# Start of a sketched-attention and ReGLU kernel: order of the first loads, filler matmuls, and the form of the stores

## Chip, cores, metric

The kernel runs on one core of a Trainium2 chip. The metric is the device time of one execution in microseconds; smaller is better. All times below are microseconds (us) unless marked otherwise, and places in a trace are counted from the start of the span.

## What is computed

Attention with polynomial sketch features, then a feed-forward layer with a gate. Cut to what matters:

```python
# q, k, v: (4 batches, 4 heads, 1088 tokens, 32); S1, S2: (8, 32), all float32
def phi(x):                                   # 64 features of a token
    a, b = S1 @ x, S2 @ x                     # 8 and 8
    return outer(a, b).reshape(64)
kv  = sum over tokens of phi(k) v^T           # per batch and head: 64 x 32
z   = sum over tokens of phi(k)
att = (phi(q) @ kv) / (phi(q) @ z + 1e-6)
x   = att, heads side by side                 # (4352 tokens, 128)
out = (relu(x @ w_gate) * (x @ w_val)) @ w_out   # d_ff = 1536, out (4352, 128)
```

## The kernel before, in words

The 4352 tokens are cut into 136 columns of 32 tokens (34 to a batch). They are worked on in nine groups: one of 8 columns, eight of 16. The feed-forward part of a group runs in "pairs": a pair is 1024 columns of hidden units times tokens, three pairs in the first group, six in each other one, 51 in all. One pair is a gate product on TensorE (gate, L553, into two PSUM tiles), two ReLU evacuations on ScalarE (relu, L566), a value product on TensorE (val, L553), their elementwise product on VectorE (prod, L570), and eight output matmuls that accumulate into o_ps (outp, L579). At the end of a group ScalarE copies o_ps to o_sb (oevac, L585), and SyncE (SP) stores it (store, L588 to L605). The first group's tokens take a quarter of the hidden units' 12 blocks of 128 in each pair, so the third pair is the first that reads blocks 8 to 11 of the gate and value weights.

Before a batch's tokens can be used, its keys go through class K (L258): transposes of k on VectorE (t1q, L319; t1r for the 64 rest keys, L315), sketches on TensorE (L330), a transpose back (t2, L350), key sums (zsum, L364), their masked copy zm on VectorE (zevac, L370), the product with S1 (w, L377) and its evacuation to wst on ScalarE (wevac, L382), the outer products that make the key features (phi, L249, on VectorE and GpSimd), and the key-value matmuls (kv, L389) with their evacuation to kv_bd (kvevac, L396). In batch 0 the value rows arrive as float32 (v32) and are cast on ScalarE (L307) ahead of wevac. A group's queries go through class Q (L418 on): transpose (L459), sketch with wst (L468), transpose back (L475), the denominator (L485 to L493), the features (L497, L249), a transpose on TensorE (tr, L509), its copy on ScalarE (L513), the product with kv_bd (num, L521) and the copy to xT (L528), which the gate product reads.

All of these, and most loads, are handed to a planner (class Plan, L21 to L76) as operations with an engine, a planned duration, dependencies and a due time. It plays them through once and emits each engine's instructions in the order of the planned starts; on the chip every engine runs its own list strictly in that order. So planned durations and landing times (the lists `land` and `qland`, L533 to L538) set orders, and only orders. Where the plan leaves TensorE idle in the head, the loop at L655 to L660 puts in filler matmuls on a tile of zeros (warm, L218 to L220); 48 more stand at the start (L222).

DMA issues before the planner (L163 to L197): the first keys on SP's and ScalarE's queues, then S1 and S2 (s16, 4 KB each), the rest keys (kR), 8 columns of q, the values; on GpSimd's queue, whose loads cast to float16, two thirds of the gate and value weights, and behind a mask two thirds of the output weights. The remaining thirds and the later batches' values are planned on GpSimd (L632 to L650), the later keys and queries on SP. The transposes of S (L225, L230) follow the 48 fillers on TensorE; skS and S1bd (L227, L232) are made of them on VectorE, ahead of the key transposes.

Of the kernel before, what the change touches and what calls it, by code (L numbers as in the profile page):

```python
# [79 lines left out]
def kernel(  # L80
# [12 lines left out]
    nc = tc.nc  # L93

    B, H, S, D = q.shape
# [4 lines left out]
    NJ = DF // 128  # L100
# [37 lines left out]
    def load_k(eng, b, h):  # L138
        eng.dma_start(out=kA[b][32 * h:32 * h + 32].rearrange("t b q d -> t b (q d)"),
                      in_=k[b, h, 0:1024, :].rearrange("(b t q) d -> t b (q d)", b=4, q=8))  # L140

    def load_kr(eng, b):
        eng.dma_start(out=kR[b], in_=k[b, :, 1024:, :].rearrange("h (t e) d -> h t (e d)", e=2))
# [5 lines left out]
    def load_vr(eng, dst, b):  # L149
        eng.dma_start(out=dst[0:64, :, 8, :], in_=v[b, :, 1024:, :].rearrange("h p d -> p h d"))  # L150
# [8 lines left out]
    def load_wo(lo, hi):  # L159
        nc.gpsimd.dma_start(  # L160
            out=wo[:, lo:hi], in_=moe_w_out.rearrange("(j f) m -> f j m", f=128)[:, lo:hi])

    load_k(nc.sync, 0, 0)  # L163
    load_k(nc.scalar, 0, 1)
    load_k(nc.sync, 0, 2)
    load_k(nc.scalar, 0, 3)
    nc.scalar.dma_start(out=s16[0:R], in_=S1[:, None, :].to_broadcast([R, 4, D]))
    nc.sync.dma_start(out=s16[R:2 * R], in_=S2[:, None, :].to_broadcast([R, 4, D]))
    load_kr(nc.sync, 0)
    nc.sync.dma_start(out=qA[:, 0:8, :],  # L170
                      in_=q[0].rearrange("h (t n) d -> h t n d", n=NT)[:, :, 0:8, :].rearrange(
                          "h t n d -> h t (n d)"))
    load_vr(nc.sync, v32, 0)

    zero = sb("zero", [128, 128], FP16)
    nc.vector.memset(zero, 0.0)
    scr = sb("scr", [1, 1], FP16)
    nc.scalar.activation(out=scr, in_=zero[0:1, 0:1], func=ACTF.Relu)
    load_v(nc.scalar, v32, 0)

    id32 = sb("id32", [2 * R, 2 * R])
    make_identity(nc, id32)
# [11 lines left out]
    load_w(wv, moe_w_val, 0, 8)  # L194
    ident = sb("ident", [128, 128], FP16)
    make_identity(nc, ident)
    load_wo(0, 8)  # L197

    z32 = sb("z32", [128, 32])
    mask2 = sb("mask2", [128, 2])  # L200
# [216 lines left out]
    class Q:  # L417


        def __init__(self, g, land):  # L420
            self.g = g
            n0, nn = self.n0, self.nn = groups[g]
            self.parts = parts(n0, nn)
            bs = [b for b, _, _ in self.parts]
            m = self.m = nn // 2
            self.qT = rot("qT", g, 4, [128, 16, 32])[:, 0:nn]
            self.ab = rot("abq", g, 4, [128, 8, 2, 32])[:, 0:m]
            self.qp = rot("qp", g, 4, [128, 8, 2, R * R], FP16)[:, 0:m]
# [12 lines left out]
            e = "DVE" if g == 0 else "POOL"  # L441
            d1 = P.add(e, 0.25 if g == 0 else 0.45, lambda: self.bwm(e), [t2])
            d2 = P.add("DVE", 0.15 + 0.15 * f, self.red, [d1])
            d3 = P.add("DVE", 0.2, self.rec, [d2])
            d4 = P.add(e, 0.25 if g == 0 else 0.42, lambda: self.am(e), [d3])
            if g == 0:
                ph = [P.add("DVE", 0.62, lambda: self.phi(0, 3, "DVE"), [d4]),
                      P.add("POOL", 0.42, lambda: self.phi(3, 4, "POOL"), [d4])]
            else:
                ph = [P.add("POOL", 0.15 + 0.226 * 4, lambda lo=lo: self.phi(lo, lo + 4, "POOL"), [d4])  # L450
                      for lo in (0, 4)]
            tr = P.add("PE", 0.47 * f, self.tr, ph, take=("M", n + "t"), lat=0.2)
            te = P.add("ACT", 0.15 + 0.85 * f, self.tre, [tr], give=(n + "t",))
            nu = P.add("PE", 0.2 + 0.25 * f, self.num, [te, *(kk[b].kvx for b in bs)],
                       take=("M", n + "x"), lat=0.25)
            self.xx = P.add("ACT", 0.15 + 0.46 * f, self.x, [nu], give=(n + "x",), due=need - 0.6)
# [73 lines left out]
                    "p (a t s) -> p a t s", a=4, s=ns),  # L530
                in_=m_ps[:, 0:32 * self.nn].rearrange("p (a s t) -> p a t s", a=4, s=ns))

    kk = [K(0, [4.8, 4.8, 4.8, 4.8, 7.2, 5.3], [0, 4, 9], [("DVE", "POOL"), ("POOL", "POOL")])]  # L533
    qland = [6.3, 16.0, 20.0, 24.0]
    qq = [Q(0, qland)]
    for b in range(1, B):
        kk.append(K(b, [[0, 14.0, 18.0, 22.0][b]] * 2, [0, 5, 9], [("POOL", "POOL")] * 2))
    qland[0] = 9.0  # L538
    for g in range(1, 9):
        qq.append(Q(g, qland))  # L540

# [45 lines left out]
    def store(g):  # L587
        n0, nn = groups[g]  # L588
        ns = nn // 4
        t = o_t.pop(g)  # L590
        runs = []
        for a in range(4):
            at = n0 + a * ns
            b, l = divmod(at, NT)
            if l + ns > NT:
                runs += [(a, 1, 0, NT - l, b, l), (a, 1, NT - l, ns, b + 1, 0)]
            elif runs and runs[-1][4] == b and runs[-1][3] == ns and runs[-1][2] == 0:
                a0, c, lo, hi, b0, l0 = runs[-1]
                runs[-1] = (a0, c + 1, lo, hi, b0, l0)
            else:  # L600
                runs.append((a, 1, 0, ns, b, l))
        for a, c, lo, hi, b, l in runs:
            dst = out[b * S:(b + 1) * S].rearrange("(t n) m -> t n m", n=NT)
            dst = dst[:, l:l + c * (hi - lo), :].rearrange("t (a s) m -> a t (s m)", a=c)
            nc.sync.dma_start(out=dst, in_=t[32 * a:32 * (a + c), lo:hi, :].rearrange("p s m -> p (s m)"))  # L605

    rel, pro, ou, oe = [], [], [], {}
    lastpe = None
    for i, (g, y) in enumerate(pairs):
# [16 lines left out]
        if lst:  # L626
            oe[g] = P.add("ACT", 0.15 + 0.42 * groups[g][1] / 16, lambda g=g: oevac(g), [ou[-1]],
                          due=due + 4.6)
            P.add("SP", 0.4, lambda g=g: store(g), [oe[g]], due=due + 5.2)


    for eng, at, fn in [  # L632
        ("POOL", 9.0, lambda: load_w(wg, moe_w_gate, 8, NJ)),
        ("POOL", 9.1, lambda: load_w(wv, moe_w_val, 8, NJ)),
        ("POOL", 9.2, lambda: load_wo(8, NJ)),
        ("POOL", 9.3, lambda: load_v(nc.gpsimd, v_sb[1], 1)),
        ("POOL", 9.4, lambda: load_vr(nc.gpsimd, v_sb[1], 1)),
    ]:
        P.add(eng, 0.6, fn, at=at, due=at + 2.0)
# [9 lines left out]
            P.add("POOL", 0.8, lambda b=b: load_v(nc.gpsimd, v_sb[b], b), at=6.0 * b, due=8.0 * b)  # L649
            P.add("POOL", 0.6, lambda b=b: load_vr(nc.gpsimd, v_sb[b], b), at=6.0 * b, due=8.0 * b)  # L650

    order = P.run({"PE": 5.0, "DVE": 4.3, "ACT": 5.2, "POOL": 5.2, "SP": 6.0})
    pe = 5.0
    go = qq[0].xx["end"]
    for o in order:  # L655
        if o["eng"] == "PE":
            if o["start"] <= go + 0.5 and o["start"] - pe > 0.3:
                warm(int((o["start"] - pe - 0.15) * 0.8 / 0.056))
            pe = o["end"]
        o["fn"]()  # L660

# [29 lines left out]
```

## Time and profile before

| what | us |
|---|---|
| median of 3 runs (lowest, highest) | 124.31 (124.18, 124.97) |
| the profiled execution's own time | 123.37 |
| its span | 121.6 |
| busy: TensorE, VectorE, ScalarE, GpSimd | 108.7, 90.0, 75.4, 52.1 |
| first gate matmul starts | 20.69 |
| last output matmuls end | 114.13 |
| last store issued | 114.8 |
| DMA packets, bytes | 10527, 9.47 MB |

The profiled execution is shorter than the three timed runs; its rows are compared with its own time. Busy time of TensorE counts pipelined matmuls whose ends are modelled, so it says little about how much of the engine is used. "PEld" is a weight load. In timelines a row gives start, duration, engine and line, output and inputs, how many instructions were merged, and in brackets how long the engine was idle before and what ended that. A row of windows gives, for a stretch of time, the busy time of each engine with its instructions, then the granted TensorE clock (1.00 is full), the DMA engines' busy share (it can exceed 1 where packets overlap) and GB/s. DMA rows give the size of one transfer and the time from issue to landing where it is known.

### The profile page before, as it was taken

Reading aid. Unit: us, or ns where it says so; the run is one execution under the profiler, and the core shown is the slowest. Engines: PE = TensorE matmul, PEld = TensorE weight load, DVE = VectorE, ACT = ScalarE, POOL = GpSimd, SP = SyncE. Lnnn points to the kernel's source line nnn. Section 1 sums busy time; section 2 is a strip of 40 time slices with the busy share of each in tenths; the row PEclk is TensorE's granted clock in tenths of the full one; section 3 lists DMA queues with packets and bytes.
Section 4 is the critical chain, followed back from the end, with each engine's and each line's share of the span. In section 5 each row is a group of like instructions: output and inputs, shape, how many; then the busy total and the mean of one; then the engine's idle time right before and its main releaser. Section 6 shows DMA issues by size and latency. Waiting matters only on the chain. (4 is left out here: it accounts for less than half of the span.)

```text
span 121.6 us, 3222 instructions
## 1 busy us (share of the span) xinstructions
PE 108.7 (89%) x1309; PEld 70.7 (58%) x1309; DVE 90.0 (74%) x145; ACT 75.4 (62%) x137; POOL 52.1 (43%) x73
## 2 busy tenths in 40 slices
PE   6968799999999999999999999989999999999300
PEld 6946578666665654665656546665666456656200
DVE  5076475977999897879989978797895897788300
ACT  2201203867867978378779754967997789897100
POOL 6619879697540189517013891260170170000000
PEclk9999558999999999999999999999999999999995
DMA  3999999999810021002001100040011021012021
GB/s 113 191 269 249 219 223 225 223 210 233 164 60 5 0 39 55 0 0 59 32 0 10 67 18 0 6 73 13 0 25 69 0 29 57 0 21 73 0 36 51
DMA packets 10527, 9.47 MB, mean 78 GB/s; under 512 B 4048, under 2 KB 8784, under 8 KB 10512
## 3 DMA queue, kind: packets, MB, share of 16 engines
q1 hardware_dynamic: 5112, 6.46, 22.9%
q0 software_dynamic: 4544, 2.02, 13.4%
q10 hardware_dynamic: 856, 0.79, 2.2%
q8 instruction: 10, 0.16, 0.6%
q14 instruction: 5, 0.04, 0.1%
HBM read 9.05 MB, written 2.23 MB: 93 GB/s over the span
## 5 line engine op out<-in xcount | busy, mean ns | idle before, releaser
L570 DVE TENSOR_TENSOR ht<-g_sb,d_ps 128x1024 f16<-128x1024 f16 x51 | 61.7, 1215 | 13.0 <-ACT g_sb L566 8.8
L566 ACT ACTIVATE g_sb<-g_ps 128x512 f16<-128x512 f32 x102 | 56.1, 598 | 14.8 <-PE g_ps L553 13.7
L579 PEld LDWEIGHTS <-ht 128*128 128x128 f16 x408 | 26.8, 113 | 11.5 <-DVE ht L570 3.0
L553 PE MATMUL g_ps<-xT,wg 128*128 128x512 f16 (+1 forms) x108 | 33.2, 368 | 0.2
L579 PE MATMUL o_ps<-wo,ht 128*128 128x128 f16 x408 | 31.4, 220 | 0.8 <-DVE ht L570 0.7
L553 PE MATMUL d_ps<-xT,wv 128*128 128x512 f16 (+1 forms) x108 | 30.3, 367 | 0.1
L249 POOL TENSOR_TENSOR kp<-abk 128x640 f16<-128x640 f32 (+1 forms) x15 | 17.8, 1212 | 6.0 <-DVE abk L350 6.0
L249 POOL TENSOR_TENSOR qp<-an,abq 128x512 f16<-128x512 f32 (+1 forms) x17 | 17.5, 1050 | 1.6 <-DVE an L497 1.0
L513 ACT COPY pt<-m_ps 128x1024 f16<-128x1024 f16 (+1 forms) x9 | 8.7, 965 | 11.0 <-PE m_ps L509 11.0
L553 PEld LDWEIGHTS <-wv 128*128 128x128 f16 x108 | 9.8, 99 | 8.5 <-issue 1.9
L485 POOL TENSOR_TENSOR bw<-abq 128x128 f32<-128x128 f32 x8 | 3.6, 456 | 24.9 <-DVE abq L475 24.9
L220 PE MATMUL o_ps<-zero 128*128 128x128 f16 x118 | 12.2, 277 | 1.1 <-DVE mask L204 1.1
L220 PEld LDWEIGHTS <-zero 128*128 128x128 f16 x118 | 10.3, 130 | 2.7 <-issue 1.3
L553 PEld LDWEIGHTS <-wg 128*128 128x128 f16 x108 | 8.6, 98 | 4.5 <-issue 1.8
L497 POOL TENSOR_TENSOR an<-abq,rd 128x128 f32<-128x128 f32 x8 | 3.3, 406 | 14.8 <-DVE rd L493 9.3
L475 DVE STREAM_TRANSPOSE abq<-d_ps 128x512 f32<-128x512 f32 (+1 forms) x9 | 6.1, 682 | 2.2 <-PE d_ps L468 2.1
L468 PE MATMUL d_ps<-qT,wst 64*64 64x256 f32 (+7 forms) x96 | 6.5, 368 | 1.2 <-ACT wst L382 1.2
L585 ACT ACTIVATE o_sb<-o_ps 128x512 f32<-128x512 f32 (+1 forms) x9 | 5.2, 572 | 2.8 <-PE o_ps L579 2.7
L459 DVE STREAM_TRANSPOSE qT<-qA 128x512 f32<-128x512 f32 (+1 forms) x9 | 5.9, 660 | 1.3 <-DMA qA<-in_q_dram 1.3
L509 PE MATMUL m_ps<-ident,qp 128*128 128x128 f16 x68 | 5.5, 224 | 0.7 <-DVE kv_bd L396 0.6
L509 PEld LDWEIGHTS <-qp 128*128 128x128 f16 x68 | 4.5, 101 | 2.4 <-issue 1.8
L528 ACT CAST xT<-m_ps 128x512 f16<-128x512 f32 (+1 forms) x9 | 5.2, 578 | 0.4 <-PE m_ps L521 0.4
(66 smaller groups left out, 70.5 us busy)
## 6 DMA issues: line engine op xcount, KB each, us to landing
kA<-in_k_dram SPq DMA_DIRECT2D x14, 128.0 KB
qA<-in_q_dram SPq DMA_DIRECT2D x12, 136.0 KB
out_dram<-o_sb SPq DMA_DIRECT2D x5, 256.0 KB
v_sb<-in_v_dram POOLq DMA_DIRECT2D x3, 256.0 KB, 9.5
v<-in_v_dram ACTq DMA_DIRECT2D x1, 512.0 KB
qA<-in_q_dram SPq DMA_DIRECT2D x4, 104.0 KB
out_dram<-o_sb SPq DMA_DIRECT2D x2, 192.0 KB
kA<-in_k_dram ACTq DMA_DIRECT2D x2, 128.0 KB
```

The source lines that it names most:

```text
L220: nc.tensor.matmul(o_ps[:, 0], zero, zero, start=True, stop=True)
L249: eng.tensor_tensor(out=dst.rearrange("p x (i j) -> p x i j", i=R), in0=a[:, :, :, None].to_broadcast([128, n, R, R]), in1=b[:, :, None, : ...
L459: nc.vector.transpose(self.qT.rearrange("p n t -> p (n t)"), qA[:, self.n0:self.n0 + self.nn].rearrange("p n d -> p (n d)"))
L468: nc.tensor.matmul(d[64 * c:64 * c + 64, hp, 32 * lo:32 * hi], wst[r, b].rearrange("p a f -> p (a f)"), self.qT[r].rearrange("p (n c) t -> ...
L475: nc.vector.transpose(self.ab.rearrange("p n a f -> p a n f"), ps(f"q{self.g}")[:, :, 0:32 * self.m].rearrange("p a (n t) -> p a n t", t=32))
L509: nc.tensor.transpose(t[:, 128 * i:128 * i + 128], self.qp[:, i].rearrange("p a f -> p (a f)"), ident)
L513: nc.scalar.copy(out=self.pt.rearrange("f n s -> f (n s)"), in_=m_ps.bitcast(FP16)[:, 0:128 * self.m])
L528: nc.scalar.copy(out=xT[:, 32 * self.n0:32 * (self.n0 + self.nn)].rearrange("p (a t s) -> p a t s", a=4, s=ns), in_=m_ps[:, 0:32 * self.nn ...
L553: nc.tensor.matmul(d[:, (y - lo) * W:(y - lo + 1) * W], w[:, js[y]], xT[:, xs], start=True, stop=True)
L566: nc.scalar.activation(out=g_t[i][:, z], in_=ps1(f"g{i}{z}"), func=ACTF.Relu)
L570: nc.vector.tensor_tensor(out=h_t[i].rearrange("p (a c) -> p a c", a=2), in0=g_t.pop(i), in1=ps(f"v{i}"), op=ALU.mult)
L579: nc.tensor.matmul(o_ps[:, s], ht[:, y * W + s:(y + 1) * W:ns], wo[:, j], start=(j == 0 and s == 0), stop=j == NJ - 1, skip_group_check=True)
```

## The change

The loads of S1 and S2 are issued first on their queues, and the first keys after them. The rest keys of batch 0 are the first load on GpSimd's queue. The values of batch 0 are issued on ScalarE's queue ahead of the activation table load. The output weights are no longer loaded in two parts of 8 and 4 blocks (the first before the planner, the second planned) but in one load of 12, planned ahead of the last third of the gate and value weights; in the built program it stands behind the three key-feature instructions of batch 0 on GpSimd. The planner's landing times, start times and SP's cost of a store are changed, and the query transpose `tr` is made to depend on kv_bd of batch 0. A gap in TensorE's plan is filled from 0.1 us on (0.3 before), with 1.1 times its length (0.8 before, less 0.15). A store is issued as pieces of 32 rows, cut where a batch ends; the last group's second and fourth go to ScalarE's queue.

What this does to the orders in the built program: fillers behind the 48 are now 16, 9, 10, 38, 2, 2, 34, 17, 14 (5, 4, 5, 5, 6, 3, 2, 22, 10, 8 before). On VectorE the key feature of batch 0 (L249) comes before zm instead of after it, the second query transpose (L459) before the first L475 instead of after it, and kv_bd before the second group's L475. On TensorE the first eight key-value matmuls come between the S1 product and the first query sketch; behind the first gate, the output matmuls of the first two pairs come together, behind the third pair's value product and the second group's num. On GpSimd the loads of the second batch's values come before the fourth part of the first query features, and the third batch's just after it. From about the fifth pair on, TensorE's order is the same. SP issues 36 store pieces and ScalarE 2; before, SP issued 15.

```diff
-    load_k(nc.sync, 0, 0)
-    load_k(nc.scalar, 0, 1)
-    load_k(nc.sync, 0, 2)
-    load_k(nc.scalar, 0, 3)
     nc.scalar.dma_start(out=s16[0:R], in_=S1[:, None, :].to_broadcast([R, 4, D]))
     nc.sync.dma_start(out=s16[R:2 * R], in_=S2[:, None, :].to_broadcast([R, 4, D]))
-    load_kr(nc.sync, 0)
+    load_kr(nc.gpsimd, 0)
+    for h in range(H):
+        load_k((nc.sync, nc.scalar)[h % 2], 0, h)
     nc.sync.dma_start(out=qA[:, 0:8, :],
...
+    load_v(nc.scalar, v32, 0)
     load_vr(nc.sync, v32, 0)
...
-    load_v(nc.scalar, v32, 0)
...
-    load_wo(0, 8)
...
-            tr = P.add("PE", 0.47 * f, self.tr, ph, take=("M", n + "t"), lat=0.2)
+            tr = P.add("PE", 0.47 * f, self.tr, [*ph, kk[0].kvx], take=("M", n + "t"), lat=0.2)
...
-    kk = [K(0, [4.8, 4.8, 4.8, 4.8, 7.2, 5.3], [0, 4, 9], [("DVE", "POOL"), ("POOL", "POOL")])]
-    qland = [6.3, 16.0, 20.0, 24.0]
+    kk = [K(0, [5.4, 5.4, 5.4, 5.4, 8.5, 5.4], [0, 4, 9], [("DVE", "POOL"), ("POOL", "POOL")])]
+    qland = [7.0, 16.0, 20.0, 24.0]
...
-    qland[0] = 9.0
+    qland[0] = 12.0
...
-        runs = []
         for a in range(4):
-            at = n0 + a * ns
-            b, l = divmod(at, NT)
...
-        for a, c, lo, hi, b, l in runs:
-            dst = out[b * S:(b + 1) * S].rearrange("(t n) m -> t n m", n=NT)
-            dst = dst[:, l:l + c * (hi - lo), :].rearrange("t (a s) m -> a t (s m)", a=c)
-            nc.sync.dma_start(out=dst, in_=t[32 * a:32 * (a + c), lo:hi, :].rearrange("p s m -> p (s m)"))
+            b, l = divmod(n0 + a * ns, NT)
+            lo = 0
+            while lo < ns:
+                hi = min(ns, lo + NT - l)
+                eng = nc.scalar if g == len(groups) - 1 and a % 2 else nc.sync
+                eng.dma_start(
+                    out=out[b * S:(b + 1) * S].rearrange("(t n) m -> t n m", n=NT)[:, l:l + hi - lo],
+                    in_=t[32 * a:32 * a + 32, lo:hi])
+                b, l, lo = b + 1, 0, hi
...
-            P.add("SP", 0.4, lambda g=g: store(g), [oe[g]], due=due + 5.2)
+            P.add("SP", 2.2, lambda g=g: store(g), [oe[g]], due=due + 5.2)
...
-        ("POOL", 9.2, lambda: load_wo(8, NJ)),
+        ("POOL", 8.9, lambda: load_wo(0, NJ)),
...
-    order = P.run({"PE": 5.0, "DVE": 4.3, "ACT": 5.2, "POOL": 5.2, "SP": 6.0})
-    pe = 5.0
+    order = P.run({"PE": 5.3, "DVE": 5.2, "ACT": 5.2, "POOL": 5.2, "SP": 4.5})
+    pe = 5.3
...
-            if o["start"] <= go + 0.5 and o["start"] - pe > 0.3:
-                warm(int((o["start"] - pe - 0.15) * 0.8 / 0.056))
+            if o["start"] <= go + 0.5 and o["start"] - pe > 0.1:
+                warm(int((o["start"] - pe) * 1.1 / 0.056))
```

More of the change, by code (lines that the diff above doesn't have):

```diff
@@ L590, in store @@
         t = o_t.pop(g)
-        runs = []
         for a in range(4):
-            at = n0 + a * ns
-            b, l = divmod(at, NT)
[L595 to L601, printed above, removed]
-        for a, c, lo, hi, b, l in runs:
-            dst = out[b * S:(b + 1) * S].rearrange("(t n) m -> t n m", n=NT)
-            dst = dst[:, l:l + c * (hi - lo), :].rearrange("t (a s) m -> a t (s m)", a=c)
-            nc.sync.dma_start(out=dst, in_=t[32 * a:32 * (a + c), lo:hi, :].rearrange("p s m -> p (s m)"))
+            b, l = divmod(n0 + a * ns, NT)
[7 more added lines that the diff above has]
+                b, l, lo = b + 1, 0, hi
     rel, pro, ou, oe = [], [], [], {}
```

## The prediction

> **What bounds the kernel now.** I read the busy slices first, then the head as a timeline, then windows of head and tail, the waits of the queues, and the landing times of the weights.
>
> ```profile
> PE   6968799999999999999999999989999999999300
> PEclk9999558999999999999999999999999999999995
> DMA  3999999999810021002001100040011021012021
> ```
>
> A slice is 3.04 us; I count them from 0. From slice 7 to slice 36 TensorE is full: 51 pairs of gate, value and output products. That middle is the same work before and after, so only three things can move: when the first gate product starts (20.69), whether the first pairs stall, and what follows the last output product (114.13). The granted clock is halved in slices 4 and 5, inside the head; the DMA engines are full up to slice 10.
>
> ```profile
> 1.06 5.05 PE L220 MATMUL o_ps<-zero 128*128 128x128 f16 x48 [1.06 <-DVE mask L204]
> ...
> 6.04 0.23 PE L225 MATMUL m_ps<-id,s 16*128 16x16 f32 x1
> ...
> 10.57 0.19 DVE L370 TENSOR_TENSOR zm<-m_ps,maskS 128x32 f32<-128x32 f32 x1 [0.30 <-PE m_ps L364]
> 10.68 1.17 DVE L249 TENSOR_TENSOR kp<-abk 128x512 f16<-128x512 f32 x1
> ...
> 11.71 1.15 ACT L307 CAST v_sb<-v 128x1152 f16<-128x1152 f32 x1 [4.87 <-DMA v<-in_v_dram]
> ...
> 12.77 0.18 ACT L382 ACTIVATE wst<-m_ps 128x16 f32<-128x16 f32 x1
> ...
> 16.30 2.53 PE L220 MATMUL o_ps<-zero 128*128 128x128 f16 x22
> ...
> 18.62 0.63 PE L509 MATMUL m_ps<-ident,qp 128*128 128x128 f16 x4
> ```
>
> In this timeline (start, duration, engine, line) the 48 filler matmuls end at 6.1, and the transpose of S starts the moment they end: the fillers hold it, not S. Later the cast of v holds ScalarE until 12.86, so wst, whose matmul ended at 11.44, is written 1.3 late. Then 22 fillers at half clock hold the feature transpose (L509) until 18.62, although kv_bd, its last condition, was done at 17.33.
>
> ```profile
> 6.00:12.50 6.50, 4.79 (x101) 3.54 (x98) 4.30 (x10) 1.09 (x2) 3.53 (x3) 1.00 1.28 257
> 12.50:19.40 6.90, 6.40 (x69) 5.12 (x70) 4.80 (x13) 0.55 (x3) 5.70 (x10) 0.51 1.22 224
> ```
>
> ```profile
> 116.00:118.00 2.00, 0.00 (x0) 0.00 (x0) 0.00 (x0) 0.00 (x0) 0.00 (x0) 1.00 0.24 31
> 118.00:120.20 2.20, 0.00 (x0) 0.00 (x0) 0.00 (x0) 0.00 (x0) 0.00 (x0) 0.58 0.23 88
> 120.20:121.60 1.40, 0.00 (x0) 0.00 (x0) 0.00 (x0) 0.00 (x0) 0.00 (x0) 0.50 0.00 1
> ```
>
> These windows end with granted clock, DMA share and GB/s. The clock is 0.51 from 12.5 to 19.4. In the tail the last store moves its data from 116.0 to 120.2 at a share of 0.23 to 0.24: four of 16 engines. SP does nothing else but wait for it:
>
> ```profile
> SPq L686 <- DMA out_dram<-o_sb: 4.8, 1, 4.8
> ```
>
> **The change, part by part.**
>
> *S first, rest keys on GpSimd.* Nothing. S has to be there at 6.04 and is held by the 48 fillers, which stay. The keys land one 4 KB load later per queue; they are read at 6.91 behind S1bd on VectorE, without a wait in the timeline. GpSimd issues the rest keys (0.70 by SP's row) before its masks: maskS moves from 2.38 to 3.1 and is read at 6.71. The weight loads start 0.7 later, before 5; their first reader is at 20.6. The rest keys are read at 8.14.
>
> *v earlier.* v is issued ahead of the table load, at about 2.2 instead of 3.35, and no output weights compete. It landed at 11.7. I take about 9; any landing before 11.4 is the same, since wst then waits for something else. The table load (1.28) moves behind the issue and ends by 4; ScalarE's next work is at 6.54.
>
> *Order of the head.* On VectorE the key feature (L249, 1.17) now runs ahead of zm, so zm goes from 10.57 to about 11.45. TensorE gets 38 fillers between the key sums and the S1 product. Fillers at full clock cost 0.05 to 0.056 each (five take 0.45, ten of the later ones 0.88 with half of them slow, 22 slow ones 2.53, or 0.11 each). So the S1 product starts at 10.6 + 38 x 0.056 = 12.75 instead of 10.82, wst ends at 13.55 instead of 12.95. Eight key-value matmuls (half of 1.17 at half clock: 0.35) lie beside the wait for wst. The query sketch starts at 13.95 (13.00 before) and lasts 0.45 at full clock instead of 0.70. VectorE: L475 0.45, then 0.23, 0.19, 0.20, 0.22, 0.56 with no transpose of 0.71 between (it moved up before the sketch): the features end at 16.45 on VectorE. On GpSimd the fourth part of the features now stands behind five issues instead of three plus one: output weights (0.77 for 4 blocks, 0.91 for 8, so 1.05 for 12), 0.60, 0.54, 0.82, 0.67 from 12.99: it starts at 16.7 and ends at 17.45. kv_bd, moved ahead of the next query's transpose, is done at 16.75. TensorE: ten key-value matmuls, 2 fillers, the second query sketch (1.13 slow, 0.65 at full), then 34 fillers of 0.056 from 15.75: 17.7. So the transpose starts at 17.7, not 18.62. After it 0.4 (0.67 slow) to the copy, 0.6 copy, the 17 fillers end at 18.9, the product, 14 fillers to 19.9. The first gate starts at 19.9 to 20.0 instead of 20.69: a gain of 0.75. Bounds: a gain of 1.2 if the fillers cost 0.05, and the loss told below if the clock falls.
>
> By the Trainium skill, page "TensorE: Matmul & The Clock Gate", section "Why this matters for your kernels", the clock falls after idle gaps over about 3 us. The row disagrees: the longest idle gap of TensorE between 6 and 12.5 is 1.22, and yet the clock was halved from 12.5. By the rule alone the clock had no reason to fall, the added fillers would buy nothing, and the head would come out at about no gain; I go by the row, which asks for a fuller TensorE.
>
> *Output weights behind the key features.* Now one load of 12 blocks is issued at 13.0, ahead of the last third of the gate and value weights. Before, those landed as follows (KB, us to landing):
>
> ```profile
> wg<-in_moe_w_gate_dram POOLq DMA_DIRECT2D x1, 128.0 KB, 5.0
> wv<-in_moe_w_val_dram POOLq DMA_DIRECT2D x1, 128.0 KB, 5.6
> wo<-in_moe_w_out_dram POOLq DMA_DIRECT2D x1, 128.0 KB, 6.6
> ```
>
> Issued at 12.95, 13.55, 14.07, the three were in at 20.7. Eight more blocks cost at least twice the 1.5 between wv and wo here, 3.0, and at most what they cost early in the head: issued at 4.11, 10.9 to landing, 6.3 behind wv. So the last value weights land between 24.0 and 27.3. GpSimd's queue moved 0.39 MB between 14 and 19; 0.64 MB at that rate end at 22.2, in at about 23.7. I take 24.2, near the lower end, because the hardware queues have less left to load by then. The third pair's value product needs them. The second pair's value product, held by VectorE's first output of 1.2, starts at 22.75 (23.61 before), the third pair's gate takes it to 23.65, so the stall is 0.55, and two pairs' output products wait behind it on TensorE. From 24.2: value 0.45, product with kv_bd 0.33, 16 output matmuls 0.9, key sums 0.7, gate 0.45, S1 product 0.6, value 0.45: the fifth pair's gate starts at 28.1, before at 28.56. So of 0.75 about 0.45 stays; I take 0.4, bounds 0.9 gain and 2.3 loss. The v load of the second batch lands three later too, at about 28; its matmuls wait for GpSimd's features, which end at 27 to 28.
>
> *Middle.* From the fifth pair TensorE's order is the same; the stores add some 1.7 of issue to each group on SP, which is past its loads at 31.35. At nothing: SP's idle hours cover it.
>
> *Stores.* The last store was one load with a leading dimension of 4 on four engines; now two pieces on SP and two on ScalarE, each of 32 rows. Issue takes 0.56 (median of 15), so the second of each queue is out 0.56 later. Data took 4.2 (116.0 to 120.2); on 16 engines 1.05. Sum: 4.2 - 1.05 - 0.56 = 2.6; I take 2.5. Bounds: 3.15 if the second issue hides, and 1.1 if the slow start (31 GB/s for 2 us in the window) stays and only the rest shrinks (2.2 to 0.55, less the issue).
>
> The Trainium skill, "DMA: Bandwidth & Descriptors", section "Bandwidth", says to batch, and that transfers under 64 KB are bound by descriptors. By its estimate of 2.0 us plus bytes over 436 GB/s a piece takes 2.15 and the whole 2.6, so four pieces would gain nothing. The row against it is the share of 0.23.
>
> **Sum.** 0.4 + 2.5 = 2.9. The profiled execution took 123.37, its span 121.6 and 1.8 around it; so 120.5 on its scale. The median of the three runs is 124.31, 0.94 more: 121.4 on that scale, which I predict.
>
> **Rivals.**
> A, the forecast, with small misses in both terms: 0.62.
> B, the stores gain only 1.1 or less, since a start of 2 us is paid by every store: 124.31 - 0.4 - 1.1 = 122.8, or 123.9 with no gain. For it: the 31 GB/s of the first two us. Against it: the four engines' share. 0.13.
> C, the weights are late: value weights at 27.3 make the head 2.3 worse than before, 124.31 + 2.3 - 2.5 = 124.1. For it: 6.3 for the eight blocks in the row. Against: that row competed with v and q. 0.12.
> D, slower: the clock falls at 12.5 all the same, and the fuller fillers run at 0.105 to 0.11 each. Then 34 of them take 3.6 instead of the 1.9 I count, 17 take 1.8, 14 take 1.5, the sketches 0.25 and 0.5 more; the first gate starts at 24.6, 3.9 later than before. With the stores: 124.31 + 3.9 - 2.5 = 125.7, with the stall hidden. It decides over the sign from a head loss of 2.5, some 60 fillers at half clock. Against it: fillers now cover nearly all of 6 to 12.5, of which TensorE was busy 4.79 of 6.5. 0.08.
> E, more than forecast, fillers short and weights in time: 124.31 - 1.2 - 3.15 = 120.0. 0.05.
>
> About 1% is what a measurement of this kernel tells from no change. Faster by more than that (under 123.07): A, E, and most of B, 0.77. Within 1%: C, the rest of B, part of D: 0.18. Slower (over 125.55): 0.05, D's worse part. The range goes from 120.2 (both terms near their best) to 123.9 (B's and C's worse halves); A's own is 120.5 to 122.4.
>
> **What would show it.** S: the transpose at L225 again starts when the 48 fillers end. Head: the granted clock at 1.0 from 6 to 20, the cast of v before 11, the 38 and 34 fillers at about 2 us each, the first gate near 20. Weights: the third pair's products wait for a DMA, and the fifth pair's gate comes at 28.1. Tail: the DMA share near 1 for about 1 us, and SP's last wait 2 instead of 4.8. Wrong, if the clock row shows 0.5 beside the fillers, if a gate or value product waits beyond 26, or if the tail from the last output product to the end (7.4 now) stays over 6.3.

## The result, and the profile after

| | before | after |
|---|---|---|
| median (lowest, highest), us | 124.31 (124.18, 124.97) | 119.08 (118.92, 123.04) |
| profiled execution, span | 123.37, 121.6 | 119.10, 117.3 |
| first gate matmul starts | 20.69 | 19.91 |
| first, last copy to o_sb ends | 31.16, 114.75 | 29.67, 113.84 |
| from there to the end of the span | 6.80 | 3.44 |

The ratio of after to before is 0.9565, 95% interval 0.9522 to 0.9608. Forecast were 121.4 and a range of 120.2 to 123.9: the direction was right, the time lies 1.1 below the range. In the profiles the difference is 4.27: 3.36 behind the last copy to o_sb and 0.91 ahead of it. The other 0.96 is that before's profiled execution was one of its shorter ones, while after's lies at its median. Of the 1.49 gained at the first copy, 0.91 is left at the last one. Ratios leave disturbed runs out, so a ratio can differ from that of two medians; and the profiled executions of after_k_first, ls_s_behind and ls_kr_four are among the longer ones of their kernels, so their rows are used for what waits for what, not for totals.

The granted clock and the DMA share of after, by slices of 2.93 us:

```profile
PEclk9999999999999999999999999999999999999995
DMA  2999999999930030002000300030002003003003
```

The half clock of slices 4 and 5 is gone. The windows of after's head (engines, then clock, DMA share, GB/s):

```profile
6.00:12.50 6.50, 5.95 (x131) 5.06 (x132) 4.82 (x11) 1.45 (x2) 3.20 (x3) 1.00 1.08 266
12.50:19.40 6.90, 6.74 (x121) 5.68 (x119) 4.84 (x13) 0.94 (x3) 6.77 (x11) 1.00 1.22 209
```

The timeline of after's head (start, duration, engine, line):

```profile
5.92 0.23 PE L222 MATMUL m_ps<-id,s 16*128 16x16 f32 x1
...
7.25 1.31 DVE L316 STREAM_TRANSPOSE kT<-kA 128x512 f32<-128x512 f32 x2 [0.38 <-DMA kA<-in_k_dram]
...
9.74 1.15 ACT L304 CAST v_sb<-v 128x1152 f16<-128x1152 f32 x1 [3.03 <-DMA v<-in_v_dram]
...
11.01 2.30 PE L217 MATMUL o_ps<-zero 128*128 128x128 f16 x38
...
13.99 0.18 ACT L379 ACTIVATE wst<-m_ps 128x16 f32<-128x16 f32 x1 [3.10 <-PE m_ps L386]
...
15.71 2.07 PE L217 MATMUL o_ps<-zero 128*128 128x128 f16 x34
...
17.62 0.39 PE L506 MATMUL m_ps<-ident,qp 128*128 128x128 f16 x4
...
19.91 0.60 PE L550 MATMUL g_ps<-xT,wg 128*128 128x256 f16 x4
```

The cast of the values starts at 9.74 instead of 11.71, yet wst comes at 13.99 instead of 12.77, since 38 fillers stand ahead of its product. Transpose and gate come where the forecast put them (17.7, 19.9 to 20.0). By this trace the head seems a small matter. The experiments say otherwise.

The tail of after, timeline, windows and SP's last wait:

```profile
113.24 0.60 ACT L582 ACTIVATE o_sb<-o_ps 128x512 f32<-128x512 f32 x1 [1.99 <-PE o_ps L576]
113.86 0.78 SPq L594 DMA_DIRECT2D out_dram<-o_sb  x2
113.87 0.85 ACTq L594 DMA_DIRECT2D out_dram<-o_sb  x2
```

```profile
114.30:114.70 0.40, 0.00 (x0) 0.00 (x0) 0.00 (x0) 0.00 (x0) 0.00 (x0) 0.97 0.09 20
114.70:115.10 0.40, 0.00 (x0) 0.00 (x0) 0.00 (x0) 0.00 (x0) 0.00 (x0) 0.50 0.86 210
115.10:115.50 0.40, 0.00 (x0) 0.00 (x0) 0.00 (x0) 0.00 (x0) 0.00 (x0) 0.50 0.97 277
115.50:116.00 0.50, 0.00 (x0) 0.00 (x0) 0.00 (x0) 0.00 (x0) 0.00 (x0) 0.50 0.50 119
116.00:116.50 0.50, 0.00 (x0) 0.00 (x0) 0.00 (x0) 0.00 (x0) 0.00 (x0) 0.50 0.00 0
```

```profile
SPq L678 <- DMA out_dram<-o_sb: 1.3, 2, 1.0
```

The data moves from about 114.7 to about 115.8, at a share of up to 0.97 where before had 0.23, and is out 2.0 behind the end of the copy to o_sb (5.4 before). Two issues take 0.78 on SP, so 0.39 each, and both queues are done with them at 114.72, about when the data begins to move.

### The profile page after: what moved, and what is told of

Its sections match the earlier page's. It is cut to its first block, busy times and chain, and to the rows that moved or that the text cites. A ratio compares the mean times of both kernels' runs of the same rounds, so it can differ in the third digit from the quotient of the medians.

```text
span 117.3 us, 3396 instructions
## 1 busy us (share of the span) xinstructions
PE 109.1 (93%) x1381; PEld 72.2 (62%) x1381; DVE 90.3 (77%) x145; ACT 75.6 (64%) x137; POOL 51.9 (44%) x73
## 5 line engine op out<-in xcount | busy, mean ns | idle before, releaser
L217 PE MATMUL o_ps<-zero 128*128 128x128 f16 x190 | 14.4, 240 | 1.1 <-DVE mask L201 1.1
L217 PEld LDWEIGHTS <-zero 128*128 128x128 f16 x190 | 12.8, 109 | 2.0 <-DVE mask L201 1.1
L465 PE MATMUL d_ps<-qT,wst 64*64 64x256 f32 (+7 forms) x96 | 5.8, 334 | 0.2 <-ACT wst L379 0.2
```

The source lines that it names most:

```text
L217: nc.tensor.matmul(o_ps[:, 0], zero, zero, start=True, stop=True)
L465: nc.tensor.matmul(d[64 * c:64 * c + 64, hp, 32 * lo:32 * hi], wst[r, b].rearrange("p a f -> p (a f)"), self.qT[r].rearrange("p (n c) t -> ...
```

## The experiments

All times are medians in us with lowest and highest. "Before" is the kernel before, run beside them: 124.3 to 124.6 in each set.

**Is the 0.94 between before's profile and its median a constant?** before_again is the kernel before once more.

> The kernel before, unchanged, for its own scatter: each run comes with its span and granted clock. Theory T (the 0.94 us between the profiled execution, 123.37, and the median of the timed runs, 124.31, is the granted clock in the head, which falls in some execution for longer than in others): the runs spread over at least 0.8 us, those with a lower mean clock are longer, and the profiled 0.959 with a span of 121.6 is at the good end. Rival U (a constant offset of timed runs): all spans within 0.3 of each other, or no relation to the clock.

Measured: 124.23 (123.54 to 125.06), ratio 0.9997 (0.9960 to 1.0034). Its profile has the first gate at 21.45 and the last copy to o_sb at 115.38, 0.76 and 0.63 later than the first profile. What differs:

```profile
12.71 1.15 ACT L307 CAST v_sb<-v 128x1152 f16<-128x1152 f32 x1 [5.76 <-DMA v<-in_v_dram]
...
13.77 0.18 ACT L382 ACTIVATE wst<-m_ps 128x16 f32<-128x16 f32 x1
```

The values land 1.0 later than in the profile that the forecast was made on (cast at 11.71, wst at 12.77). The signs of theory T are there: the runs spread over 1.5, and the five with the lowest granted clock average 124.6, the five with the highest 123.9. So the 0.94 is no constant but scatter, and by these two profiles it arises ahead of the first gate. Late values and a low clock come together in them, so which of the two makes it is not shown.

**The stores alone, and after without them.**

```diff
# stores_only: before, with the new loop of pieces (L587 to L597 of after)
# after_old_stores: after, with the old loop (L588 to L605 of before)
```

> The kernel before with only the body of the store function changed to pieces of 32 rows. From the traces, the stretch from the last output product to the end went from 7.42 to 4.07. T: the tail is worth 3.3 to 3.4 by itself and nothing else moves, so 120.9 to 121.0. U (the stores also free time in the middle, by shorter stays on the DMA engines): more than 4, under 120.3. My prediction's term, 2.5, would give 121.8.

> The changed kernel with the old body of the store function. T: 119.08 + 3.4 = 122.4 to 122.5, the head's gain untouched and the median again equal to the profiled execution within 0.3. U: 123.1 or more.

Measured: stores_only 120.85 (120.62 to 121.03), ratio 0.9725 (0.9684 to 0.9767); after_old_stores 122.53 (121.79 to 127.03), ratio 0.9841 (0.9789 to 0.9893). The stores are worth 3.46 on before's head (124.31 - 120.85) and 3.45 on after's (122.53 - 119.08). The forecast had 2.5. What is left for all the rest is 1.8 (120.85 - 119.08), where the forecast had 0.4.

**All four last pieces on SP.**

```diff
-                eng = nc.scalar if g == len(groups) - 1 and a % 2 else nc.sync
+                eng = nc.sync
```

> After, with the last group's four pieces all on SP's queue. An issue of a piece of 32 rows takes SP 0.39, so the fourth is out 0.78 later than with two queues, and landing takes 1.7 whichever queue it is: 119.08 + 0.8 = 119.9 (119.6 to 120.1). Rival: the pieces share the queue's engines so that the issue is hidden behind the data of the earlier ones, 119.0 to 119.3. The other way: a queue alone takes four engines for all four pieces, as the one big store did, and the tail is as long as before, 122 or more.

Measured: 119.82 (119.52 to 121.22). Four issues in one row:

```profile
113.82 1.72 SPq L594 DMA_DIRECT2D out_dram<-o_sb  x4
```

1.72 instead of 0.78 of issue, and 0.74 more in the time. The second queue is worth about that; the rest of the tail's gain is the pieces themselves.

**Do the fuller fillers bring the head's gain?** Once undone in after, once alone on before.

```diff
# after_old_fillers (before_new_fillers the other way round, on before)
-            if o["start"] <= go + 0.5 and o["start"] - pe > 0.1:
-                warm(int((o["start"] - pe) * 1.1 / 0.056))
+            if o["start"] <= go + 0.5 and o["start"] - pe > 0.3:
+                warm(int((o["start"] - pe - 0.15) * 0.8 / 0.056))
```

> The changed kernel with the old rule for filler matmuls (48, 10, 4, 5, 25, 23, 10, 8 instead of 48, 16, 9, 10, 38, 2, 2, 34, 17, 14), all orders as in the changed kernel. T: the clock falls again for part of the head, runs spread with their clock, and the median is 1.0 to 2.0 longer, 120.1 to 121.1. U (the fillers are dead weight ahead of the S1 product and the feature transpose): 0.3 to 0.8 shorter, 118.3 to 118.8.

> The kernel before with only the new rule for fillers (48, 10, 9, 10, 10, 11, 7, 6, 34, 17, 14). If the half clock of the head cost the kernel before its time, and fillers cure it: the granted clock stays at 1.0 in the head, and 123.0 to 123.6. If the fillers are dead weight, or TensorE still idles while wst waits for the cast of the values, and the clock falls all the same: 124.5 to 126.5.

Measured: after_old_fillers 118.72 (117.99 to 120.08); before_new_fillers 124.50 (123.68 to 125.82), ratio 1.0031 (0.9989 to 1.0072). Undone they cost nothing (0.36 less, within the scatter); alone they bring nothing. The windows of before_new_fillers:

```profile
6.00:12.50 6.50, 5.10 (x114) 4.21 (x115) 4.14 (x10) 0.30 (x1) 2.83 (x3) 1.00 1.23 251
12.50:19.40 6.90, 5.95 (x109) 4.89 (x107) 4.08 (x13) 1.66 (x3) 5.79 (x9) 1.00 1.22 218
```

The clock is full through the head, and yet its first gate is at 20.84, since the cast of the values starts at 12.65. Against before_again, with the half clock and as late a cast (12.71), the gate is 0.6 earlier, but the first product (L570) is not, 23.10 and 22.98: VectorE waits 1.34 for the next queries ahead of it. In this execution what the full clock gained was lost again to late queries.

**The planner's times.** after_old_plan takes back the landing and start times and the added condition of `tr`, and with them the new orders.

```diff
-            tr = P.add("PE", 0.47 * f, self.tr, [*ph, kk[0].kvx], take=("M", n + "t"), lat=0.2)
+            tr = P.add("PE", 0.47 * f, self.tr, ph, take=("M", n + "t"), lat=0.2)
-    kk = [K(0, [5.4, 5.4, 5.4, 5.4, 8.5, 5.4], [0, 4, 9], [("DVE", "POOL"), ("POOL", "POOL")])]
+    kk = [K(0, [4.8, 4.8, 4.8, 4.8, 7.2, 5.3], [0, 4, 9], [("DVE", "POOL"), ("POOL", "POOL")])]
# and qland, and the start times of P.run, likewise
```

> The changed kernel with the planner's old landing and start times and without the new dependency of the query transpose: the orders of the engines in the head are those of before (zm ahead of the key feature; the second batch's values behind the first query features on GpSimd), with the new loads and the new filler rule (48, 10, 9, 10, 10, 11, 7, 6, 34, 17, 14). T2: the values are in early, so wst is written right after the S1 product, near 11.8; the head is shorter than in the changed kernel and the first gate comes at 18.6 to 19.4: 118.0 to 118.8. U2 (the new orders carry the gain): 119.8 to 120.8.

Measured: 118.74 (118.27 to 120.65), ratio 0.9580 (0.9542 to 0.9618). Nothing lost. The new orders bring the first copy forward, but from its end to that of the last copy it takes 84.2 in every profile with them and 83.6 in every one with the old orders, this one included, so that part is not kept. So neither fillers nor orders bring the gain; the load edits remain.

**The loads alone; loads and stores without the rest.** loads_only is before with the four load edits of the diff (S first, rest keys on GpSimd, values ahead of the table load, output weights in one load behind the key features), old plan, old fillers, old stores. loads_stores has the new stores too.

> The kernel before with the four load edits alone: S1 and S2 first, rest keys on GpSimd's queue, values of batch 0 issued ahead of the table load, output weights as one load of 12 blocks behind the key features. The planner's times, the filler rule, the query transpose and the stores are those of before. The stores alone took 124.3 to 120.85, and the whole change reaches 119.08, so 1.5 to 1.8 is to be found in the head; the fuller fillers alone gave nothing, and taking back the planner's times lost nothing. Theory L (the loads carry the head's gain): 122.3 to 122.9, with the cast of the values done before wst's matmul (it ends after 12 in most traces of before) and the first gate at 19.2 to 20.2. Rival N (the loads give nothing by themselves; the head's gain belongs to the shorter tail or to the two together): 123.8 to 124.6, first gate above 20.5.

> The loads and the stores of after, with the planner's times, the query transpose and the filler rule of before. Theory L: loads and stores are all that counts, and the fuller fillers are dead weight of 0.3 to 0.4 in the end: 118.0 to 118.7, the first gate at 18 to 19. Rival: the fuller fillers and the new orders help each other, and without both the head is as before: 120.5 to 121. A third way: the same as after, 118.9 to 119.3, if the later waits (values of the second batch, keys) give the earlier gate back in full.

Measured: loads_only 121.06 (120.49 to 122.39), ratio 0.9712 (0.9648 to 0.9777); loads_stores 118.62 (117.38 to 119.22), ratio 0.9498 (0.9409 to 0.9587). The loads alone are worth 3.2 (124.31 - 121.06), eight times the forecast's 0.4 and more than theory L's 122.3; together with the stores they come out where theory L put them. The timeline of loads_only:

```profile
8.24 1.15 ACT L304 CAST v_sb<-v 128x1152 f16<-128x1152 f32 x1 [1.49 <-DMA v<-in_v_dram]
...
11.39 0.18 ACT L379 ACTIVATE wst<-m_ps 128x16 f32<-128x16 f32 x1 [1.99 <-PE m_ps L374]
...
17.49 0.60 PE L550 MATMUL g_ps<-xT,wg 128*128 128x256 f16 x4
```

The cast is over long before wst's product; wst waits for that product alone (1.99, PE), and the first gate is 3.2 earlier than before. loads_stores has it at 18.00, after at 19.91: new orders and fillers put 1.9 of it on again, of which 0.83 is left at the last copy to o_sb (113.01 and 113.84) and 0.46 in the medians, less than these runs separate.

**Which load edit?** First out of after, then out of loads_stores, one at a time.

```diff
# after_wo_early, ls_wo_early: eight blocks of the output weights early again
+    load_wo(0, 8)
-        ("POOL", 8.9, lambda: load_wo(0, NJ)),
+        ("POOL", 9.2, lambda: load_wo(8, NJ)),
# after_v_late, ls_v_late: load_v(nc.scalar, v32, 0) behind the table load again
# after_k_first: keys, then S1 and S2, then rest keys on SP, as before
# ls_s_behind: keys, then S1 and S2; rest keys stay on GpSimd
# ls_kr_on_sp: S1 and S2, keys, then rest keys on SP
-    load_kr(nc.gpsimd, 0)
+    load_kr(nc.sync, 0)
```

> The changed kernel with the output weights loaded as before, two thirds of them early on GpSimd's queue, the last third behind the last gate and value weights. T2 (the head was freed because batch 0's values land by 9.7 instead of 11.7, and they do so since no output weights compete): the values land 1.5 to 2.5 later, their cast ends at 12.4 to 13.4, and with the S1 product done at 13.7 that costs 0 to 0.3: 119.1 to 119.4. U2 (the weights late in the queue hold the first pairs, and loading them early is better): 118.3 to 118.8. My prediction counted a stall of 0.35 from this part.

> The changed kernel with batch 0's values issued behind the activation table load again. T2: 1.3 to 1.5 later issue, landing at about 10.5 to 11, the cast ends before the S1 product does, the rest keys and keys land earlier because the values no longer compete (the first key transpose waited 0.38 for a DMA): no loss, 118.7 to 119.1. U2 (the early issue is what shortens the head): 0.8 or more longer, from 119.9.

> After, with the keys first on their queues, S1 and S2 behind them and the rest keys on SP's queue, as before. My prediction priced that part at nothing, since 48 fillers hold the transpose of S: 118.9 to 119.3. Rival: S first or the shorter SP queue is what brings the values early (they are read by the cast ahead of wst), then wst comes 1 or more later and the time is 119.8 to 120.6.

> loads_stores with the rest keys back on SP's queue behind the keys; the weight loads on GpSimd's queue then start at 2.3 instead of 3.7. Theory G (the rest keys' place is what counts: on SP they land late, as in after_k_first, where the transpose L312 waited 3.08 for them, and the earlier weight loads compete with the values): the transpose of the rest keys waits for a DMA, the cast of the values starts at 10.5 or later, 119.8 to 121. Rival S (S first is what counts): 118.2 to 119.0, and the cast before 10.

> loads_stores with S1 and S2 behind the keys of their queues, the rest keys still first on GpSimd's. Theory G: nothing, 118.2 to 119.0, since the 48 fillers hold the transpose of S until 5.3 to 6. Rival S: 119.8 to 121, with the transpose of S waiting for a DMA beyond 6.2.

> loads_stores with the values issued behind the table load. If the place of the values is worth nothing (the cast ran at 8.71 with it taken back in after): 118.2 to 119.1, the cast before 10. If it is a part of the head's gain: 119.3 to 120.3, with wst held by the cast (cast later than 10.7).

> loads_stores with eight blocks of the output weights loaded early on GpSimd's queue, four later. If these compete with the values and the later keys: 119.2 to 120.2, with the cast at 10 or later or the second batch's key transpose waiting for its DMA. If not: 118.2 to 119.0.

| kernel | undone | time | cast of v starts | first gate |
|---|---|---|---|---|
| after | - | 119.08 | 9.74 | 19.91 |
| after_wo_early | output weights late | 119.74 (119.31 to 120.31) | 9.44 | 19.12 |
| after_v_late | values early | 120.24 (119.16 to 123.64) | 8.71 | 20.16 |
| after_k_first | S first, rest keys | 120.97 (119.89 to 124.03) | 11.15 | 24.97 |
| loads_stores | - | 118.62 (117.38 to 119.22) | 9.19 | 18.00 |
| ls_kr_on_sp | rest keys on GpSimd | 122.38 (120.89 to 122.79) | 12.15 | 21.80 |
| ls_s_behind | S first | 119.40 (118.80 to 120.60) | 11.44 | 19.75 |
| ls_v_late | values early | 118.40 (117.08 to 119.07) | 9.41 | 17.68 |
| ls_wo_early | output weights late | 119.04 (118.53 to 120.17) | 8.47 | 17.25 |

The rest keys are the edit that counts: 32 KB on SP's queue instead of GpSimd's cost about 3. That is 3.0 by the ratios to before (0.9743, 0.9667 to 0.9819, against 0.9498), 2.7 in the two profiles (last copy to o_sb at 115.74 and 113.01), and 3.8 in the medians (122.38 - 118.62), which lie above theory G's 121. The values' place is worth nothing by ls_v_late (118.40); after_v_late leaves it open (120.24, but from 119.16 on, with the cast earlier than in after). S first (0.8) and the late output weights (0.4 and 0.7) a little, in medians whose ranges overlap or nearly do. The timeline of ls_kr_on_sp, with its clock:

```profile
9.57 0.24 DVE L312 STREAM_TRANSPOSE kT<-kR 128x64 f32<-128x64 f32 x1 [1.40 <-DMA kR<-in_k_dram]
...
12.15 1.15 ACT L304 CAST v_sb<-v 128x1152 f16<-128x1152 f32 x1 [5.35 <-DMA v<-in_v_dram]
...
14.44 0.18 ACT L379 ACTIVATE wst<-m_ps 128x16 f32<-128x16 f32 x1 [1.14 <-PE m_ps L374]
```

```profile
6.00:12.50 6.50, 4.02 (x83) 3.03 (x81) 3.12 (x8) 0.65 (x2) 1.85 (x2) 0.73 0.86 217
12.50:19.40 6.90, 6.90 (x74) 5.36 (x73) 5.09 (x11) 0.98 (x2) 5.42 (x8) 0.51 0.97 184
```

VectorE waits 1.40 for the rest keys themselves, then the values land 3 later than in loads_stores, and here the clock falls too. The values hold up SP's own list as well: it issues the next batch's keys only after a wait, in ls_kr_on_sp of 5.4 and in loads_stores of 1.0 (line waited for, total, times, longest):

```profile
SPq L139 <- DMA v<-in_v_dram: 5.4, 1, 5.4
```

```profile
SPq L139 <- DMA v<-in_v_dram: 1.0, 1, 1.0
```

Before had this wait at 3.5, after has it at 1.8. In ls_kr_on_sp it lasts until 12.08; the second batch's keys, transposed at 17.73 in loads_stores, are transposed at 20.39.

after_k_first shows what fuller fillers do when the clock falls all the same. Its rest keys come at 10.59 after a wait of 3.08, TensorE stands idle for 3.19, and the 38 fillers that take 2.30 in after then take:

```profile
14.47 3.90 PE L217 MATMUL o_ps<-zero 128*128 128x128 f16 x38
```

That execution is the one of 124.03. It is the forecast's rival D in small (38 fillers at 0.103 each), on one execution of one kernel.

**How do the rest keys delay the values, and are they enough alone?** before_kr_pool makes this one edit on before. ls_kr_four leaves the rest keys on SP, as four loads of 32 rows instead of one whose leading dimension is 4.

```diff
# ls_kr_four
-    load_kr(nc.sync, 0)
+    for h in range(H):
+        nc.sync.dma_start(out=kR[0][32 * h:32 * h + 32],
+                          in_=k[0, h, 1024:, :].rearrange("(t e) d -> t (e d)", e=2))
```

> Before, with the rest keys of batch 0 on GpSimd's queue, first there, and nothing else changed. If this edit carries the head's gain by itself: 121.2 to 122.5, the cast of the values before 11, the first gate at 18 to 19.5. If it needs the others with it (the early output weights, or the keys behind S): 123.3 to 124.6, the cast beyond 11.4.

> ls_kr_on_sp with the rest keys as four loads of 32 rows on SP's queue instead of one whose leading dimension is 4; the weight loads still start at 2.3. Theory F (the one load runs on four engines, and the values' packets on these engines wait behind it): the rest keys are there when VectorE wants them, the cast starts before 10.5, 118.6 to 119.8. Theory W (the earlier weight loads take the engines from the values): the cast stays at 11 or later, 121 to 122.8.

Measured: before_kr_pool 124.43 (121.76 to 125.62), ratio 0.9891 (0.9816 to 0.9965); ls_kr_four 124.22 (123.34 to 126.36), ratio 0.9980 (0.9933 to 1.0027). ls_kr_four does not decide between the two theories. The four issues end only at 4.46, the queries and the last 64 rows of the values behind them on SP go out later still, and VectorE waits 3.00 for the rest keys. The cast starts at 11.72, but it needs two loads: 512 KB that ScalarE issues and those last rows, 32 KB that SP issues at 6.05. The small load landed at 11.65 (5.6 behind its issue); for the large one the profile has no landing. Theory F's 118.6 to 119.8 and theory W's 121 to 122.8 are both missed.

The two loads have to be told apart elsewhere too. These are their rows in ls_s_behind, size and time to landing:

```profile
v<-in_v_dram ACTq DMA_DIRECT2D x1, 512.0 KB, 5.4
v<-in_v_dram SPq DMA_DIRECT2D x1, 32.0 KB, 7.5
```

Issued at 2.38 and 3.92, they were in at 7.78 and 11.42, and the cast started at 11.44: it waited for the small load. So it did in after_k_first (large in at 9.95, small at 11.08, cast at 11.15). In ls_kr_on_sp (12.08, cast at 12.15) and stores_only (13.01 against 11.46, cast at 13.07) it waited for the large one. So rest keys on SP go with late values in two ways. SP issues its 32 KB of values at 3.30 to 6.05, against 2.54 to 2.59 with the rest keys on GpSimd (3.92 in ls_s_behind, where S stands ahead). And where the landing is known, the large load takes 7.6 to 9.8, against 5.4 to 7.4. The second fits weight loads competing with the values: in every profile here the first weight load starts at 2.3 when the rest keys are on SP and at 3.7 when they are on GpSimd. These things move together in all these kernels, though. Rest keys on SP with the weights held back by 1.4, or with SP's values ahead of them, were not run, so which way carries the time is open.

before_kr_pool is the more instructive one. Its first gate is the earliest of all, and its first product is not. Here is before_kr_pool, then loads_only:

```profile
17.20 0.60 PE L553 MATMUL g_ps<-xT,wg 128*128 128x256 f16 x4
...
20.57 1.30 DVE L459 STREAM_TRANSPOSE qT<-qA 128x512 f32<-128x512 f32 x2 [2.50 <-DMA qA<-in_q_dram]
...
21.79 1.18 DVE L570 TENSOR_TENSOR ht<-g_sb,d_ps 128x1024 f16<-128x1024 f16 x1
```

```profile
17.49 0.60 PE L550 MATMUL g_ps<-xT,wg 128*128 128x256 f16 x4
...
18.57 1.26 DVE L456 STREAM_TRANSPOSE qT<-qA 128x512 f32<-128x512 f32 x2
...
19.76 1.18 DVE L567 TENSOR_TENSOR ht<-g_sb,d_ps 128x1024 f16<-128x1024 f16 x1
```

VectorE, whose order is fixed, stands 2.50 at the query transposes that come ahead of the first product, because the next queries are late; the first copy to o_sb ends at 32.06, later than in before (31.16). So the gate's 3.5 is given back in that execution. Of the timed runs little is left: the median is 0.1 below before's 124.56 beside it, and the ratio of 0.9891 goes by only three of ten runs. With the other load edits beside it the queries are there (loads_only: 28.72). loads_stores has no such wait either. With the output weights early again (ls_wo_early), or S behind the keys (ls_s_behind), it is back, in one execution each:

```profile
19.87 1.31 DVE L457 STREAM_TRANSPOSE qT<-qA 128x512 f32<-128x512 f32 x2 [1.41 <-DMA qA<-in_q_dram]
```

```profile
21.77 1.30 DVE L456 STREAM_TRANSPOSE qT<-qA 128x512 f32<-128x512 f32 x2 [2.48 <-DMA qA<-in_q_dram]
```

The edits bring their 3.2 together: the rest keys' place opens the head, and S first and the late output weights go with queries that come in time. Why the queries come earlier with them is not shown.

## Why the prediction was wrong

The forecast was 2.33 too long. Of this 0.86 is the stores (3.36 in the profiles against 2.5), 0.51 what is ahead of the last copy (0.91 against 0.4), and 0.96 the step from the profiled execution to the median.

Right were the direction, the parts the time would come from, and the places in the head: the transpose of S when the 48 fillers end (5.92), the feature transpose at 17.62 (17.7), the first gate at 19.91, rival B's slow start refuted. Four steps were not.

- **"S first, rest keys on GpSimd": "Nothing."** This is the step whose mechanism failed. It went by the readers of what moved (rest keys at 8.14, no wait) and not by what shares the queues with it. The rest keys' place alone moves the time by about 3 once the rest is as in loads_stores, and it was priced at nothing. The weight loads start 1.4 later with it (2.31 and 3.69), not 0.7. The forecast had the values in at about 9 because they are issued earlier and no output weights compete; with either of these undone the cast still starts at 8.47 to 9.44, while with the rest keys on SP it starts at 11.15 or later. So the values came about when forecast (9.68) for another reason, and that the first gate is where the forecast put it is luck to that extent. The forecast's "any landing before 11.4 is the same" was true for wst and overlooked SP, whose next key loads wait for v.
- **"The median of the three runs is 124.31, 0.94 more."** This was carried over as a constant, and it is the largest piece of the miss. It is none: before_again's profile lies 0.30 below its median, stores_only's 0.23, after's 0.02 above. The forecast was made on a short execution of before: the values are cast at 11.71 in it, and at 12.65, 12.71 and 13.07 in three other profiles with that load order (before_new_fillers, before_again, stores_only). That the changed kernel gains more against a usual execution of before than against this one fits its early values, and would be why the head counts 1.8 in the medians and 0.91 in the two profiles. It is not shown that the change removes the scatter: after's own runs go from 118.92 to 123.04.
- **The stores, 2.5.** The mechanism was right, the term mis-sized: 3.36 in the profiles, 3.45 in the medians. The forecast subtracted 0.56 for a second issue; it takes 0.39 to 0.42 and ends about when the data begins to move, so it hides, and the data itself took about 1.1, as said. That is the case of the forecast's upper bound, 3.15, which was 0.2 short.
- **The 0.35 taken off for late weights (a stall of 0.55).** It did not come. The last value weights were issued at 14.93 and landed 8.2 later, at 23.1 instead of 24.2, and the third pair's value product, which needs them, started at 23.59 without a wait for a DMA.

In rival D the terms listed add up to 4.0 on a gate at 20.0, so to a first gate at 24.0 and about 125.1, not 24.6 and 125.7.

What the fillers were worth was wrong too, though it cancelled: the forecast's "I go by the row, which asks for a fuller TensorE" is not borne out. Taken back they lose nothing, alone they gain nothing. The Trainium skill, "TensorE: Matmul & The Clock Gate", section "Part 1: The HAM clock gate", says that the clock is decided in free-running windows of 3.4 us, so that where it changes differs from run to run. These runs agree that it differs: the same 48 fillers at the start lasted from 4.11 to 5.30 us in the profiles. The length of the window cannot be read from them. The forecast's row, one execution with the half clock from 12.5, was one draw.

The Trainium skill, "DMA: Bandwidth & Descriptors", section "Why a DMA increments its semaphore by 16 and not by 1", has the number of engines follow from the slowest dimension of the access pattern. The last store of before, with a leading 4, agrees (a share of 0.23 of 16 engines); pieces of 32 rows reached 0.97. For the rest keys, with a leading 4 as well, the same thought led to theory F, which no run here settles, since in ls_kr_four the small load of values is what the cast waited for.

In sum: 3.5 of the 5.2 are the stores, 1.8 the loads, less what new orders and fillers take back. No version here is shown to be faster than after: loads_stores (118.62), ls_v_late (118.40), after_old_fillers (118.72) and after_old_plan (118.74) lie below it, with overlapping ranges.

## What to carry to other kernels

When a small load is moved to another queue, price what stands behind it on both queues and what competes with it, not only its reader: 32 KB moved the time by about 3. Where an instruction needs two loads, ask for each of them when it lands and what stands ahead of it. Make the sum against several profiles of the kernel before, since a single one can be a short execution, and its distance from the median need not carry over to the changed kernel. And an earlier start is worth only what the next loads allow: look for the first instruction behind it that waits for a DMA.

## What was not expected of the hardware

- The last group's data is out 2.0 after it is written when it goes as four pieces of 32 rows on two queues, and 5.4 after when it goes as one piece with a leading dimension of 4.
- The half clock came with TensorE's longest idle gap at 1.22 (before) and stayed away with a gap of 1.9 (loads_stores, behind the second row of fillers). A gap of 3.19 (after_k_first) went with a fall, and so did one of 1.8 (ls_kr_on_sp), so the longest gap alone does not tell.
- An issue on SP can stand for microseconds behind a load of other data on another queue: 5.4 for the next batch's keys, behind the values that ScalarE had issued.
